# Sums of w_out in parts within block 0, and the copy of v with k^T v within the second product of block 1

## Chip, cores and metric

The kernel runs on one core of a Trainium2 chip. The metric is the device time of one execution in microseconds (us). A core has five engines with a queue of instructions each: TensorE (PE in the profile; its weight loads are PEld), VectorE (DVE), ScalarE (ACT), GpSimd (POOL) and SyncE (SP). Each works through its own queue in order and waits for the others by semaphores. Transfers are issued by SP and POOL here and run on 16 DMA engines.

## What is computed

A linear attention with cosine weights, whose result goes through a feed-forward layer with a quick gelu. Everything arrives and leaves as float32; the kernel computes the products in bf16.

```python
# q, k, v: 8 batches x 8 heads x 576 positions x 64
def phi(x, c, s):
    r = np.maximum(x, 0.0)
    return np.concatenate([r * c, r * s], axis=-1)
q_p = phi(q, cos_w, sin_w)
k_p = phi(k, cos_w, sin_w)
kv = np.einsum('bhsf,bhsd->bhfd', k_p, v)
z = np.sum(k_p, axis=2)
num = np.einsum('bhsf,bhfd->bhsd', q_p, kv)
den = np.einsum('bhsf,bhf->bhs', q_p, z)[..., None] + 1e-06
attn_out = num / den
# x: attn_out as 4608 tokens x 512; w_in 512 x 2048, w_out 2048 x 512
h = x @ w_in
g = h * (1.0 / (1.0 + np.exp(-1.702 * h)))
return g @ w_out
```

## The kernel before

A block is one batch: 576 positions, of which 512 are its main tokens and 64 its tail. The tails of all blocks are gathered and computed at the end. The scheduler is off: each engine runs its instructions in the order in which the program writes them, so a line's place in the source is its place in the queue of its engine.

For each block b there are these steps:

- `trig_q(c)` (L176) makes the q features of one of five chunks of positions, a cosine and a sine half each, on VectorE (or ScalarE with `act`), from the loaded `qf` into `qn`; `qturn_dma(c)` (L217) turns the chunk into `qT` by a DMA transpose that SP issues.
- `trig(kr, kf, j)` (L161) makes the k features of one of nine slices `j`, two halves each, from the loaded `kf` into `kr`: on VectorE, on ScalarE with `act=True`, and with `act="sin"` the sine half alone on ScalarE.
- `vcopy(i0, i1, act)` (L187) casts v from `vf` to bf16 in `vt`, for the pairs of heads i0 to i1, on VectorE or on ScalarE.
- `kv_next()` (L589) is k^T v: 72 matmuls on TensorE from `kr` and `vt` into a PSUM tile `at`, and its evacuation to `kvs` on VectorE (`kv_evac`, L243).
- `x_next(b, c)` (L759) makes x of one chunk: `num_mm` (8 matmuls from `qT` and `kvs`), `num_div` (three VectorE instructions ending in `xn`), and `xturn_dma`, a DMA transpose from SP into `xT` (chunks 0 to 3) or `xt` (the tail).
- `mm1(b, fc)` (L373) is the first product for 128 of the 2048 hidden columns: 4 matmuls of 128x512 on TensorE, then a gelu on ScalarE into `g`. Its PSUM tiles come from the pool `pmm` of four banks, so mm1 of column group n writes where column group n-4 was, and waits for that one's gelu.
- The second product of blocks 1 to 7 uses seven smaller products in place of eight (`PRODUCTS`, L473: p1, p2, p6, p5, p7, p3, p4, of 16 matmuls in each of two steps). It needs sums of parts of w_out (`wsum`: t1, t2, t3, nt4, made once in `w_sums`, L438) and sums of parts of g for each block (`sums`: s1 to s4, made in `g_sums`, L458, for half h = 0 or 1 of the column groups). s3 of half h reads the gelus 4h to 4h+3, the others those and 8+4h to 11+4h. `wino_after` (L549) keeps or joins results after each product and stores them.

Block 0 uses the plain second product (`mm2`, L414). While it runs, block 1's q, k and v are prepared (L716 to L728); then `start_block(1)` runs mm1 of the first five column groups of block 1, and `w_sums()` stands after it (L765). The loop over blocks 1 to 7 (L767) runs mm1 over the other column groups with the preparation of block b+1 written in between, and then the second product. Within that product, for b = 1, `vcopy()` is written after step 1, k^T v of the next block after step 3, and the five `x_next` after steps 4, 5, 6, 8 and 10. For b > 1 k^T v is written between mm1 of groups 13 and 14.

w_out is loaded in four groups of 4 of its 16 row blocks by POOL (`load_wout`, L150). k and v of a later block are loaded by SP (`load_kv`, L146), q by SP too (`load_q`, L133). Block 2's loads are issued at L727 and L728; block 3's q is issued in the loop of block 1, after block 2's qT transposes, and its k and v after the fourth `x_next`.

Of the kernel before, what the change touches and what calls it, by code (L numbers as in the profile page):

```python
# [15 lines left out]
SUB = mybir.AluOpType.subtract  # L16
# [4 lines left out]
def kernel(  # L21
# [9 lines left out]
    nc = tc.nc  # L31
# [29 lines left out]
    kf, vf = [one.tile([128, NI, S], F32, name=n) for n in ("kf", "vf")]  # L61
# [47 lines left out]
    kr = one.tile([128, NS, NI, 128], BF16, name="kr")  # L109
# [17 lines left out]
    def load_chunks(t, src, b, eng):  # L127
        eng.dma_start(out=t[:, 0:2048].rearrange("p (h e) -> p h e", h=H),
                      in_=src[b, :, 0:512, :].rearrange("h (p c) d -> p h (c d)", c=4))
        eng.dma_start(out=t[0:64, 2048:2560].rearrange("p (h e) -> p h e", h=H),  # L130
                      in_=src[b, :, 512:S, :].rearrange("h p d -> p h d"))

    def load_q(b, eng=nc.gpsimd):  # L133
        load_chunks(qf, q, b, eng)
# [11 lines left out]
    def load_kv(b):  # L146
        load(kf, k, b, nc.sync)
        load(vf, v, b, nc.sync)
# [12 lines left out]
    def trig(dst, src, j, act=False, eng=nc.vector):  # L161

        i = src[:, :, ts(j, 64)]
        for cs, w in enumerate((cosw, sinw)):
            o = dst[:, j, :, ts(cs, 64)]
            if act is True or (act == "sin" and cs == 1):
                nc.scalar.activation(o, i, AF.Relu, scale=w[:, j:j + 1])
            else:
                eng.tensor_scalar(o, i, 0.0, w[:, j:j + 1], op0=MAX, op1=MUL)  # L169
# [6 lines left out]
    def trig_q(c, act=False):  # L176
        n = 128 if c < 4 else 64
        i = chunk(qf, c)
        for cs, w in enumerate((cosw, sinw)):
            o = qn[0:n, c, :, ts(cs, 64)]  # L180
            sc = w[0:n, NS + c:NS + c + 1]
            if act:
                nc.scalar.activation(o, i, AF.Relu, scale=sc)
            else:
                nc.vector.tensor_scalar(o, i, 0.0, sc, op0=MAX, op1=MUL)  # L185

    def vcopy(i0=0, i1=NI, act=False):  # L187
        o = vt[:, :, i0:i1, 0:64].rearrange("p j i e -> p i j e")
        i = vf[:, i0:i1].rearrange("p i (j e) -> p i j e", e=64)
        if act:  # L190
            nc.scalar.activation(o, i, AF.Copy)
        else:
            nc.vector.tensor_copy(o, i)  # L193
# [23 lines left out]
    def qturn_dma(c):  # L217
        n = 128 if c < 4 else 64
        nc.sync.dma_start_transpose(out=qT[:, :, c * 128:c * 128 + n],
                                    in_=qn[0:n, c].rearrange("p h f -> p (h f)"))  # L220
# [3 lines left out]
    def kv_open(i0=0, i1=NI, n=65):  # L224
        t = pat.tile([128, 2, 512], F32, name="at")
        for i in range(i0, i1):
            st["kv", i] = t[:, :, ds((i - i0) * n, n)]
        st["ps", i0] = t[:, :, 0:(i1 - i0) * n]
        if i0 == 0:
            st["kvs"] = small.tile([128, 2, NI, VW], BF16, name="kvs", bufs=2)  # L230

    def kv_mm(i0, i1, rhs, col, n):
        for i in range(i0, i1):
            for j in range(NS):
                for hh in range(2):
                    r = slice(hh * 64, hh * 64 + 64)
                    nc.tensor.matmul(st["kv", i][:, hh, ds(col, n)], kr[r, j, i, :], rhs(r, i, j),  # L237
                                     start=(j == 0), stop=(j == NS - 1))
# [4 lines left out]
    def kv_evac(i0, i1, n=65):  # L243
        o = st["kvs"][:, :, i0:i1, 0:n]
        nc.vector.tensor_copy(o, st["ps", i0].rearrange("p hh (i e) -> p hh i e", e=n))  # L245
# [85 lines left out]
    def x_open(b):  # L331
        x[b] = xpool.tile([128, KC, MT], BF16, name="xT")
# [40 lines left out]
    def mm1(b, fc):  # L373
        mm1_part(b, fc, 0, MT)
        gelu(fc)
# [38 lines left out]
    def mm2(b, t, lo, hi, c0=0, c1=d_model, end=False):  # L414
# [6 lines left out]
        if hi == FC:  # L421
# [10 lines left out]
    wt = {n: wsum[:, i].rearrange("p (f d) -> p f d", f=HF)  # L432
          for i, n in enumerate(("t1", "t2", "t3", "nt4"))}
    wq = {(k, n): w_out_sb[:, ts(k, HF), ts(n, HD)] for k in range(2) for n in range(2)}
    sg = {n: sums[:, i].rearrange("p (f t) -> p f t", f=HF)
          for i, n in enumerate(("s1", "s2", "s3", "s4"))}

    def w_sums():  # L438
        tt = nc.vector.tensor_tensor
        tt(wt["t1"], wq[0, 1], wq[0, 0], op=SUB)  # L440
        tt(wt["t2"], wq[1, 1], wt["t1"], op=SUB)
        tt(wt["t3"], wq[1, 1], wq[0, 1], op=SUB)
        tt(wt["nt4"], wq[1, 0], wt["t2"], op=SUB)

    def main_blk(i, qd):

# [11 lines left out]
    def g_sums(names, h, of=MAIN):  # L458

        tt = nc.vector.tensor_tensor  # L460
        a_blk, to = of
        o = {n: to[n][:, ts(h, 4)] for n in to}
        for n in names:
            if n == "s1":
                tt(o[n], a_blk(1, h), a_blk(1, h + 2), op=ADD)
            elif n == "s2":
                tt(o[n], o["s1"], a_blk(0, h), op=SUB)  # L467
            elif n == "s3":
                tt(o[n], a_blk(0, h), a_blk(1, h), op=SUB)  # L469
            else:  # L470
                tt(o[n], a_blk(0, h + 2), o["s2"], op=SUB)
# [114 lines left out]
    def vt_rhs(r, i, j):  # L586
        return vt[r, j, i, 0:65]

    def kv_next():  # L589
        kv_open()  # L590
        kv_mm(0, 4, vt_rhs, 0, 65)
        kv_evac(0, 4)

    def start_block(b):
# [120 lines left out]
    load_wout(3)  # L715
    for j in range(NS):  # L716
        trig(kr, kf, j)
    for fc in range(8, FC):
        mm1(0, fc)
    mm1_tail_first(0)  # L720
    mm1_tail_first(1)
    for c in range(5):
        trig_q(c, act=(c > 2))
        qturn_dma(c)
    vcopy(0, 2)
    vcopy(2, 4, act=True)
    load_q(2, nc.sync)  # L727
    load_kv(2)  # L728
    for g in range(2):
# [2 lines left out]
    for t in range(4):  # L732
        mm2(0, t, 8, 12)
    kv_next()
    mm2(0, 0, 12, 16)
    x_open(1)
# [15 lines left out]

    def kv_operands(b):
        for j in range(NS):
            trig(kr, kf, j)
        if b > 2:
            vcopy()

    def x_next(b, c):  # L759
        num_mm(c)  # L760
        num_div(c)
        xturn_dma(b, c)


    w_sums()  # L765

    for b in range(1, B):  # L767
        nb = b + 1 if b + 1 < B else None
        f0 = 5 if b == 1 else 0
        for fc in range(f0, FC):  # L770
            if nb is not None and fc == f0:
                for c in range(5):
                    trig_q(c)
                    qturn_dma(c)
            if nb is not None and fc == f0 + 1:
                kv_operands(nb)

                if nb + 1 < B:
                    load_q(nb + 1, nc.sync)
            if fc == 12:  # L780
                g_sums(("s3",), 0)
                g_sums(("s3",), 1)
                g_sums(("s1", "s2", "s4"), 0)
            if fc == 14 and nb is not None and b > 1:
                kv_next()
            mm1(b, fc)
        if nb is not None:
            x_open(nb)
            if b > 1:
                x_next(nb, 0)  # L790
            g_sums(("s1", "s2"), 1)
            at = {2 * p + 1: [p + 1] for p in range(4)} if b > 1 else {4: [0], 5: [1], 6: [2], 8: [3], 10: [4]}
            wino_open()
            for p in range(7):
                for c in range(2):
                    wino_mm(p, c)
                    s = 2 * p + c
                    if c == 1:
                        wino_after(b, p)
                    if s == 3 and b == 1:  # L800
                        kv_next()
                    for c2 in at.get(s, ()):
                        x_next(nb, c2)
                        if c2 == 3 and nb + 1 < B:
                            load_kv(nb + 1)
                    if s == 1:
                        g_sums(("s4",), 1)
                        if b == 1:
                            vcopy()
            continue  # L810
        for fc in range(FC):
            mm1_tails(fc)
            if fc == 0:
                g_sums(("s1", "s2", "s4"), 1)
        for h in range(2):
            g_sums(("s1", "s2"), h, TAIL)
        g_sums(("s3",), 0, TAIL)
        g_sums(("s3",), 1, TAIL)
        wino_open()
        for p in range(7):  # L820
            for c in range(2):
                wino_mm(p, c, TAIL)
            wino_after(None, p, end=True)
            if p == 1:
                g_sums(("s4",), 0, TAIL)
                g_sums(("s4",), 1, TAIL)
        wino_open(last=True)
        for p in range(7):
            for c in range(2):
                wino_mm(p, c)  # L830
                if p == 6:
                    wino_last(b, c)
            wino_after(b, p, end=True)
# [30 lines left out]
```

## Time and profile before

| What | Value |
|---|---|
| median of 3 runs | 286.86 us (286.69 to 287.23) |
| time of the profiled execution | 288.89 us |
| span of the profiled execution | 287.2 us |
| mean granted TensorE clock | 0.987 |
| busy: PE, DVE, ACT, POOL | 273.7, 185.7, 128.3, 41.4 us |
| bytes read from and written to HBM | 36.70 MB, 9.44 MB |

The span runs from the first to the last instruction of the trace; all moments named below count from its start. Block 1's second product begins at 65.54 us, block 2's mm1 at 88.66 us.

How to read the lines. A timeline line gives start, duration, engine, source line, operation, the tiles written and read, their shapes, a count, and in brackets the idle time of the engine before it with what ended it. A line of waits gives who waited for whom, the sum in us, how often, and the longest. A line of windows gives the stretch, its length, busy time and count of PE, PEld, DVE, ACT and POOL, then the granted clock, the busy share of the DMA engines and GB/s. A line of DMA issues gives tiles, issuing queue, count, size and the time from issue to landing (a median where several are grouped). L numbers are lines of the kernel before.

### The profile page before, as it was taken

What the parts mean: (1) busy time and instruction counts of PE and PEld (TensorE: products, weight loads), DVE (VectorE), ACT (ScalarE), POOL (GpSimd) and SP (SyncE); (2) the same over time, 40 slices, a digit from 0 to 9 for tenths busy, and PEclk for the clock granted to TensorE, in tenths of its full rate; (3) what the DMA queues carried; (4) which work ended last, traced back from release to release, by engine and by line L of the source; (5) the groups of instructions that cost most, each with busy time, mean ns of one, the idle gap of its engine ahead of it and who ended that gap; (6) DMA issues with size and microseconds to landing.
All of it is one profiled execution on the core that took longest, in us unless ns stands there. A gap on an engine that the chain in (4) does not pass through costs nothing.

```text
span 287.2 us, 6573 instructions
## 1 busy us (share of the span) xinstructions
PE 273.7 (95%) x2700; PEld 191.5 (67%) x2700; DVE 185.7 (65%) x451; ACT 128.3 (45%) x225; POOL 41.4 (14%) x70
## 2 busy tenths in 40 slices
PE   8999999996698989999999999999999999999995
PEld 2675645854594559757975797579757975568884
DVE  4835434799585798796779678967897711516111
ACT  6967543672014722364236413641374137773221
POOL 5680003200112001300130013001300130000320
PEclk9999999999599999999999999999999999999999
DMA  7999999999349999999699979987994430000143
GB/s 238 245 212 295 270 257 204 350 296 202 103 64 251 290 183 168 292 264 236 112 305 221 217 148 314 256 212 107 290 279 54 109 119 2 0 0 2 47 138 110
DMA packets 73661, 53.57 MB, mean 187 GB/s; under 512 B 52736, under 2 KB 63488, under 8 KB 73632
## 3 DMA queue, kind: packets, MB, share of 16 engines
q1 hardware_dynamic: 67504, 36.97, 56.8%
q0 software_dynamic: 6128, 16.19, 20.2%
q8 instruction: 21, 0.34, 0.5%
q14 instruction: 8, 0.07, 0.1%
HBM read 36.70 MB, written 9.44 MB: 161 GB/s over the span
## 4 chain that ended last, share of the span: by engine, by line
PE 77%; DVE 10%; DMA 9%; issue 1%; ACT 1%; POOL 0%; DVEq 0%; SPq 0%
PE mm L502 32%; PE mm L365 29%; DMA kf<-in_k_dram 5%; PE mm L396 4%; PE mm L419 4%; PE at L237 3%; DVE kr L169 3%; PE at L310 3%; DMA sums<-in_v_dram 2%; DMA out_dram<-ysb 2%; DVE qn L185 1%; DVE vt L193 1%; DVE sums L469 1%; PE mm L388 1%; DVE sums L467 1%
## 5 line engine op out<-in xcount | busy, mean ns | idle before, releaser
L365 PE MATMUL mm<-xT,w_in 128*128 128x512 bf16 (+1 forms) x592 | 113.7, 349 | 1.5 <-DMA xT<-xn 1.4
L371 ACT ACTIVATE g<-mm 128x512 bf16<-128x512 f32 x128 | 75.6, 598 | 41.2 <-PE mm L365 41.2
L365 PEld LDWEIGHTS <-w_in 128*128 128x128 bf16 x592 | 60.1, 113 | 48.3 <-issue 1.7
L502 PEld LDWEIGHTS <-sums 128*128 128x128 bf16 x448 | 42.6, 98 | 5.0
L508 POOL DMA_DIRECT2D out_dram<-ysb x24 | 17.5, 729 | 165.2 <-DVE inv L323 96.8
L502 PE MATMUL mm<-wsum,sums 128*128 128x256 bf16 x336 | 40.9, 276 | 0.0
L502 PEld LDWEIGHTS <-g 128*128 128x128 bf16 x336 | 32.2, 98 | 3.8
L169 DVE TENSOR_SCALAR kr<-kf,cosw 128x256 bf16<-128x256 f32 x69 | 24.2, 350 | 10.0 <-DMA kf<-in_k_dram 10.0
L325 DVE TENSOR_TENSOR xn<-at,inv 128x512 bf16<-128x512 f32 x39 | 27.0, 691 | 1.3
L502 PE MATMUL mm<-w_out_sb,g 128*128 128x256 bf16 x224 | 26.4, 272 | 0.0
L169 DVE TENSOR_SCALAR kr<-kf,sinw 128x256 bf16<-128x256 f32 x68 | 23.1, 339 | 0.0
L517 ACT ACTIVATE kept_u<-mm 128x512 f32<-128x512 f32 (+1 forms) x9 | 4.9, 550 | 33.7 <-PE mm L502 16.9
L517 ACT ACTIVATE kept_p<-mm 128x512 f32<-128x512 f32 (+1 forms) x17 | 9.7, 572 | 22.6 <-PE mm L502 22.6
L185 DVE TENSOR_SCALAR qn<-qf,cosw 128x512 bf16<-128x512 f32 (+1 forms) x33 | 16.3, 494 | 4.0 <-DMA qf<-in_q_dram 4.0
L321 DVE TENSOR_SCALAR den<-at 128x8 f32<-128x8 f32 x36 | 5.9, 163 | 17.4 <-PE at L310 17.4
L310 PEld LDWEIGHTS <-qT 128*128 128x128 bf16 x312 | 14.6, 98 | 3.4 <-issue 1.0
L569 ACT ACTIVATE ysb<-mm 128x512 f32<-128x512 f32 x6 | 3.6, 597 | 29.3 <-PE mm L502 29.3
L310 PE MATMUL at<-kvs,qT 128*128 128x65 bf16 x312 | 15.9, 194 | 0.8 <-DVE kvs L245 0.8
L237 PEld LDWEIGHTS <-kr 64*128 64x128 bf16 x576 | 10.3, 98 | 8.2 <-issue 6.5
L185 DVE TENSOR_SCALAR qn<-qf,sinw 128x512 bf16<-128x512 f32 (+1 forms) x33 | 15.6, 473 | 0.0
L237 PE MATMUL at<-vt,kr 64*128 64x65 bf16 x504 | 9.7, 197 | 5.5 <-DVE vt L193 5.5
L419 PE MATMUL mm<-w_out_sb,g 128*128 128x512 bf16 x64 | 14.8, 379 | 0.0
(120 smaller groups left out, 264.7 us busy)
## 6 DMA issues: line engine op xcount, KB each, us to landing
kf<-in_k_dram SPq DMA_DIRECT2D x6, 1152.0 KB, 6.5
vf<-in_v_dram SPq DMA_DIRECT2D x6, 1152.0 KB, 11.8
qf<-in_q_dram SPq DMA_DIRECT2D x6, 1024.0 KB, 6.5
out_dram<-ysb POOLq DMA_DIRECT2D x24, 256.0 KB, 6.5
w_out_sb<-in_moe_w_out_dram POOLq DMA_DIRECT2D x4, 512.0 KB, 17.6
kf<-in_k_dram POOLq DMA_DIRECT2D x1, 1152.0 KB, 13.2
vf<-in_v_dram POOLq DMA_DIRECT2D x1, 1152.0 KB, 20.7
w_in<-in_moe_w_in_dram POOLq DMA_DIRECT2D x2, 512.0 KB, 10.2
```

The source lines that it names most:

```text
L169: eng.tensor_scalar(o, i, 0.0, w[:, j:j + 1], op0=MAX, op1=MUL)
L185: nc.vector.tensor_scalar(o, i, 0.0, sc, op0=MAX, op1=MUL)
L237: nc.tensor.matmul(st["kv", i][:, hh, ds(col, n)], kr[r, j, i, :], rhs(r, i, j), start=(j == 0), stop=(j == NS - 1))
L310: nc.tensor.matmul(ps[:, h // 4, ds((h % 4) * 65, 65)], qT[:, h, ts(c, 128)], kvs_of(h), start=not eps_too, stop=(not eps_too or h % 4 == ...
L325: nc.vector.tensor_tensor(xn, pv[:, :, :, 0:64], inv.unsqueeze(3).to_broadcast([128, 2, 4, 64]), op=MUL)
L365: nc.tensor.matmul(hp[fc][:, t0:t1], wcol(kc, fc), x[b][:, kc, t0:t1], start=(kc == 0), stop=(kc == KC - 1))
L371: nc.scalar.activation(gT[fc // 4][:, fc % 4], hp.pop(fc), AF.Gelu_apprx_sigmoid)
L396: nc.tensor.matmul(hps[:, 64:B * 64], wcol(kc, fc), xt[:, kc, 64:B * 64], start=(kc == 0), stop=(kc == KC - 1))
L419: nc.tensor.matmul(yp[b, t, c0][:, c0:c1], w, w_out_sb[:, fc, c0:c1], start=(fc == 0), stop=(fc == FC - 1))
L502: nc.tensor.matmul(bank[to][c], lhs, rhs, start=opens, stop=(fc == HF - 1), skip_group_check=True)
L508: eng.dma_start(out=dst[:, 2 * i + c0:2 * i + c1, ts(n, HD)], in_=t[:, c0:c1])
L517: nc.scalar.activation(o, i, AF.Identity)
```

## The change

The four sums of w_out are no longer made in one go after `start_block(1)`. t1 is made behind block 0's k features; t2, t3 and nt4 are made in two halves, the first behind block 1's q features, the second behind VectorE's half of the copy of v. In block 1 (b == 1) the two s3 sums and the k features of block 2 move behind mm1 of group 7, with the sine half of every second slice on ScalarE; s4 of half 0 leaves the place at group 12. The copy of v is written ahead of the second product, half on ScalarE and half on VectorE. k^T v stays behind step 3, with the two s4 sums around its evacuation. The `x_next` stand behind steps 5, 6, 7, 8 and 10. Blocks 2 to 7 keep their order.

```diff
-    def w_sums():
+    def w_sum_1():
+        nc.vector.tensor_tensor(wt["t1"], wq[0, 1], wq[0, 0], op=SUB)
+
+    def w_sums(h):
+
         tt = nc.vector.tensor_tensor
-        tt(wt["t1"], wq[0, 1], wq[0, 0], op=SUB)
-        tt(wt["t2"], wq[1, 1], wt["t1"], op=SUB)
-        tt(wt["t3"], wq[1, 1], wq[0, 1], op=SUB)
-        tt(wt["nt4"], wq[1, 0], wt["t2"], op=SUB)
+        o = {n: wt[n][:, ts(h, 4)] for n in wt}
+        w = {n: wq[n][:, ts(h, 4)] for n in wq}
+        tt(o["t2"], w[1, 1], o["t1"], op=SUB)
+        tt(o["t3"], w[1, 1], w[0, 1], op=SUB)
+        tt(o["nt4"], w[1, 0], o["t2"], op=SUB)
...
-    def kv_next():
+    def kv_mm_next():
         kv_open()
         kv_mm(0, 4, vt_rhs, 0, 65)
+
+    def kv_next():
+        kv_mm_next()
         kv_evac(0, 4)
...
     for j in range(NS):
         trig(kr, kf, j)
+    w_sum_1()
     for fc in range(8, FC):
         mm1(0, fc)
...
     for c in range(5):
         trig_q(c, act=(c > 2))
         qturn_dma(c)
+    w_sums(0)
     vcopy(0, 2)
     vcopy(2, 4, act=True)
+    w_sums(1)
     load_q(2, nc.sync)
     load_kv(2)
...
     def kv_operands(b):
         for j in range(NS):
-            trig(kr, kf, j)
+            trig(kr, kf, j, act="sin" if b == 2 and j % 2 else False)
         if b > 2:
             vcopy()
...
-    w_sums()
 
     for b in range(1, B):
...
-            if nb is not None and fc == f0 + 1:
+            if nb is not None and fc == f0 + 1 and b > 1:
                 kv_operands(nb)
 
                 if nb + 1 < B:
                     load_q(nb + 1, nc.sync)
-            if fc == 12:
+            if fc == 8 and b == 1:
+                load_q(nb + 1, nc.sync)
                 g_sums(("s3",), 0)
                 g_sums(("s3",), 1)
-                g_sums(("s1", "s2", "s4"), 0)
+                kv_operands(nb)
+            if fc == 12:
+                if b > 1:
+                    g_sums(("s3",), 0)
+                    g_sums(("s3",), 1)
+                g_sums(("s1", "s2", "s4") if b > 1 else ("s1", "s2"), 0)
...
             g_sums(("s1", "s2"), 1)
-            at = {2 * p + 1: [p + 1] for p in range(4)} if b > 1 else {4: [0], 5: [1], 6: [2], 8: [3], 10: [4]}
+            if b == 1:
+                vcopy(2, 4, act=True)
+                vcopy(0, 2)
+            at = ({2 * p + 1: [p + 1] for p in range(4)} if b > 1 else
+                  {5: [0], 6: [1], 7: [2], 8: [3], 10: [4]})
...
-                    if s == 3 and b == 1:
-                        kv_next()
                     for c2 in at.get(s, ()):
                         x_next(nb, c2)
                         if c2 == 3 and nb + 1 < B:
                             load_kv(nb + 1)
-                    if s == 1:
+                    if s == 1 and b > 1:
                         g_sums(("s4",), 1)
-                        if b == 1:
-                            vcopy()
+                    if s == 3 and b == 1:
+                        kv_mm_next()
+                        g_sums(("s4",), 0)
+                        kv_evac(0, 4)
+                        g_sums(("s4",), 1)
```

## The prediction

> **What bounds the kernel now.** I read the page first, then the list of waits and the timeline of PE between 40 and 122 us, then windows by stage for the clock, and last VectorE, SP and the DMA landings of that stretch. The page gives the frame: PE works almost throughout.
>
> ```profile
> PE 273.7 (95%) x2700; PEld 191.5 (67%) x2700; DVE 185.7 (65%) x451; ACT 128.3 (45%) x225; POOL 41.4 (14%) x70
> PE   8999999996698989999999999999999999999995
> PEclk9999999999599999999999999999999999999999
> ```
>
> PE is full from the third slice on, except slices 10 and 11 (each slice is 7.18 us, so 65 to 79 us), and slice 11 is the only one with a low granted clock. From 118 us on the chain of waits is PE alone and each block takes 28.57 us (one block's p1 to the next). So a change to blocks 0 and 1 can only act on what stands before 118 us. The waits of PE between 24 and 125 us, and PE's timeline around them:
>
> ```profile
> PE at L237 <- DVE vt L193: 5.5, 2, 4.8
> PE mm L365 <- DMA xT<-xn: 1.4, 1, 1.4
> PE at L310 <- DVE kvs L245: 0.8, 1, 0.8
> ```
> ```profile
> 65.54 3.66 PE L502 MATMUL mm<-w_out_sb,g 128*128 128x256 bf16 x32
> 74.05 2.16 PE L237 MATMUL at<-vt,kr 64*128 64x65 bf16 x72 [4.85 <-DVE vt L193]
> 76.14 1.89 PE L502 MATMUL mm<-wsum,sums 128*128 128x256 bf16 x8
> ...
> 88.66 12.25 PE L365 MATMUL mm<-xT,w_in 128*128 128x512 bf16 x56 [1.41 <-DMA xT<-xn]
> ```
> ```profile
> 66.00:74.00 8.00, 3.20 (x30) 2.72 (x28) 7.86 (x16) 0.94 (x2) 0.00 (x0) 0.84 0.84 201
> 74.00:90.00 16.00, 14.54 (x199) 12.26 (x199) 11.37 (x29) 2.06 (x4) 3.00 (x4) 0.87 0.47 91
> 106.00:119.00 13.00, 13.00 (x144) 11.72 (x142) 9.86 (x23) 1.79 (x3) 2.18 (x3) 1.00 0.97 212
> ```
>
> After four steps of the second product (p1, p2) PE stands for 4.85 us until VectorE has copied v. Then it runs slowly: the 72 k^T v matmuls take 2.16 us (1.19 between the same marks of the chain in later blocks), the first step behind them 1.82 (0.87 elsewhere). The granted clock, the column before the last two, is 0.84 and 0.87 there and 1.00 later. VectorE is why:
>
> ```profile
> 53.98 1.22 DVE L440 TENSOR_TENSOR wsum<-w_out_sb 128x2048 bf16<-128x2048 bf16 x1
> ...
> 58.65 0.48 DVE L185 TENSOR_SCALAR qn<-qf,cosw 128x512 bf16<-128x512 f32 x1
> ...
> 72.64 1.35 DVE L193 CAST vt<-vf 128x2304 bf16<-128x2304 f32 x1
> ```
>
> From 53.98 to 73.99 it never idles: w_sums 4.67 us, trig_q 3.96, the 18 kr instructions 4.7, the sums of g 5.3, the copy 1.35. What the stall costs: the second product of block 1 is 14 steps of 0.873, k^T v 1.19 and five num_mm of 0.24, together 14.6 us; begun at 65.54 it would end at 80.2. The trace ends it at 87.25 (88.66 less 1.41). So 7.05 us are at stake: 5.0 of standing (from the end of step four at 69.03) and 2.05 of low clock.
>
> **The change, part by part.** *w_sums out of block 1 (VectorE).* The four sums leave the 4.67 us before trig_q. t1 goes behind block 0's kr work, which ends at 31.3; it needs groups 0 and 1 of w_out, landed at 14.14 + 14.8 = 28.9 and 14.69 + 16.6 = 31.3. It takes 1.22 us, to 32.6; VectorE idles until q lands at 35.38, so it costs nothing (2.8 us of cover). The first half of t2, t3, nt4 stands behind trig_q, which ends at 37.8; group 2 lands at 19.52 + 18.4 = 37.9; three instructions of 128x1024 at 0.61 (the row of L465) end at 39.8, before v lands at 40.84: nothing. The second half needs group 3, the last of the four loads:
>
> ```profile
> w_out_sb<-in_moe_w_out_dram POOLq DMA_DIRECT2D x1, 512.0 KB, 19.6
> ```
>
> Issued at 23.73, it lands at 43.33; 1.9 us of sums end at 45.25, and the evacuation of kvs behind them, for which num_mm waits, began at 45.24 before. Cost 0 to 0.1 here, and if group 3 came 1 us later, 1 us at that place; I take 0 because, as follows, block 1 waits for a landing anyway.
>
> *trig_q, then s3, then kr.* trig_q can start at 54.07 (q landed at 46.84 + 7.2 = 54.04) and ends at 58.0. The first s3 sum runs to 58.6; the second waits for gelu 7, which ends at 59.44, and is done at 60.1. kr needs the k of block 2, whose issue on SP and time to landing are:
>
> ```profile
> 48.57 0.64 SPq L125 DMA_DIRECT2D kf<-in_k_dram  x1
> ```
> ```profile
> kf<-in_k_dram SPq DMA_DIRECT2D x1, 1152.0 KB, 12.1
> ```
>
> It lands at 48.57 + 12.1 = 60.67, which w_sums hid before (first kr at 62.61). Now two engines wait for it: VectorE 0.6 us (hidden), and ScalarE, where four sine halves stand between gelu 7 and gelu 8. ScalarE's Relu instructions of this shape followed each other at 0.40 us (L167, 6.88 to 12.46), so they run 60.71 to 62.31, and gelu 8, which started at 59.76, ends at 62.9. Behind it queue all later gelus, and mm1 has four banks: mm1(12), due at 62.27, needs gelu 8's. PE stands some 0.65 us and mm1 ends at 66.2 instead of 65.54. Were k there at 59.4, this would be nothing; each further microsecond of k is a microsecond.
>
> [...]
>
> *kr, sums, copy.* VectorE's 14 kr instructions (0.263 apart) end at 64.4. s1, s2 of half 0 need gelu 11 (ScalarE catches up at 0.5 per gelu: 64.4) and end at 65.8; s1, s2 of half 1 need gelu 15 (67.05) and end at 68.5. The copy is split: ScalarE's half 1.17 us from 66.95 to 68.1 (v lands at 49.38 + 14.4 = 63.8), VectorE's 0.76 from 68.4 to 69.15. PE finishes p2 at 66.2 + 3.5 = 69.7: 0.55 us of cover, so the 4.85 us and the low clock go. keep("p1") is pushed to 68.1 behind ScalarE's copy, and its bank is wanted at 70.9. The two s4 sums now stand around the kvs evacuation: join to 70.4, s4 to 71.0, kvs to 71.7, s4 to 72.3; kvs is wanted at 72.64, s4 at p3 (77.1). No stall.
>
> *num_mm one step later.* PE: k^T v to 70.9, p6 to 72.64, then num_mm 0 to 3 one step (1.11 us) apart, the fourth ending at 76.2, the product at 80.85. xn of the fourth ends 1.33 later (82.48 to 83.81 before): 77.55. SP's transposes take 1.2 to 1.3 us each from 74.25, so the fourth is issued at 78.15, or at 79.2 if the third takes 2.28 again. Landing 3.9 later (84.6 to 88.5 before): 82.05 to 83.1. I take 82.5 for mm1 of block 2, against 88.66.
>
> *SP.* block 2's five qT transposes are issued from 55.0 instead of 59.6, behind k and v in the same queue; load_q(3) follows, wanted at 79. The loads of block 3 follow the fourth xT transpose as before, so block 2 keeps its own two waits (0.6 and 0.8 us).
>
> **Sum.** 7.05 recovered, less 0.65 (gelu 8) and 0.25 more of waiting for xT: 6.15, that is 88.66 - 82.5. The profiled execution took 288.89 us with a span of 287.2; the median of the runs is 286.86, 0.3 below the span. I subtract from the median: 280.7 us.
>
> **Rivals.** *The transposes slow k (slower).* If the DMA engines shared their time between the early qT transposes and k and v, k's remaining 5.7 us at 55.0 would double (five transposes are 6.5 us of work at 1.3 each): k at 66.4. ScalarE's queue would then hold gelu 8 until 68.6, PE would stand 6.4 us at mm1(12), longer than the 4.85 that brought the low clock (another 2.05): 8.45 lost against 7.05 won, and with 0.25 for xT 288.5 us. It decides from a k some 4 us late. Against it: block 2's xt transpose, issued at 87.38 behind v (86.72), landed 11.8 later at 99.2, and v at 98.9; the quickest took 2.3. The queue kept its order. [...] *xT comes late.* With four transposes one step apart, the longest landing in the xT rows (6.2) would give 78.15 + 6.2 + 0.15 = 84.5 and 282.7 us. *More is won.* If k of block 3 lands after 6.0 as in the next block instead of 9.5, block 2's waits of 0.6 and 0.8 go too: 279.3. Against it, the same three stores run beside it. *It doesn't do what it says.* If VectorE's half of the copy were still last, by more than the 0.55, PE would stand for the rest; for no gain at all it would have to be 6 us late, and no row on its way is so uncertain, except k.
>
> **Chances.** Forecast (280.0 to 281.8) 0.65; xT late or a similar wait of 1 to 2 us 0.14; more won 0.12; slower by the transposes 0.06; no gain 0.03. The range takes the first three but for their edges: 279.1 to 283.0. A measurement of this kernel tells 0.2% (0.6 us) from no change: faster 0.91, same 0.02, slower 0.07.
>
> **What would show it.** PE's timeline: no wait before the k^T v of block 1, and 72 matmuls in 1.2 us; a short wait at L365 inside block 1's mm1; clock 1.00 in the slice at 74 us; mm1 of block 2 near 82.5 with a wait for xT of 1 to 2 us. ScalarE: four L167 rows that start at 60.7 behind a wait for kf. VectorE: wsum between 31 and 46 us. Wrong would be kf landing past 62, a long wait at L365, or vt still as PE's releaser.

## The result and the profile after

The changed kernel takes 282.69 us in the median of four runs (282.08 to 283.27), the kernel before 287.05 beside it (286.69 to 287.61): a ratio of 0.9846 with a 95% interval of 0.9818 to 0.9875, that is 4.4 us less (3.6 to 5.2). The profiled execution has a span of 280.3 us. Two repeats of the same kernel gave ratios of 0.9823 (0.9770 to 0.9877) and 0.9827 (0.9775 to 0.9880). Disturbed runs are left out of all comparisons; the profiled execution of both these repeats was one, so they give times and no trace.

The page of the changed kernel, TensorE's share and the granted clock by slice:

```profile
PE 271.2 (97%) x2700; PEld 190.0 (68%) x2700; DVE 184.5 (66%) x450; ACT 130.6 (47%) x230; POOL 41.4 (15%) x70
...
PE   7899999999989999999999999999999999999994
...
PEclk9999999999999999999999999999999999999999
```

The hole in slices 10 and 11 is gone and the clock with it; what is left is an 8 in the twelfth, at 77 to 84 us (each slice is 7.0 us). PE's waits between 24 and 125 us, then its timeline:

```profile
PE mm L365 <- DMA xT<-xn: 1.2, 1, 1.2
PE at L310 <- DVE kvs L245: 0.8, 1, 0.8
PE mm L365 <- ACT g L371: 0.4, 1, 0.4
PE at L237 <- DVE vt L193: 0.2, 1, 0.2
```
```profile
62.67 3.61 PE L365 MATMUL mm<-xT,w_in 128*128 128x512 bf16 x16 [0.37 <-ACT g L371]
66.12 3.66 PE L507 MATMUL mm<-w_out_sb,g 128*128 128x256 bf16 x32
69.71 1.26 PE L237 MATMUL at<-vt,kr 64*128 64x65 bf16 x72
...
82.20 12.25 PE L365 MATMUL mm<-xT,w_in 128*128 128x512 bf16 x56 [1.18 <-DMA xT<-xn]
94.63 1.26 PE L237 MATMUL at<-vt,kr 64*128 64x65 bf16 x72 [0.18 <-DVE vt L193]
...
98.50 0.40 PE L310 MATMUL at<-kvs,qT 128*128 128x65 bf16 x8 [0.75 <-DVE kvs L245]
```

k^T v now follows the fourth step with no wait. The row of 72 k^T v matmuls lasts 1.26 us where it lasted 2.16, and block 1's second product takes 14.9 us (66.12 to 81.02, which is 82.20 less 1.18) in place of 21.7. (A step of it is 8 matmuls, as the row of 32 for four steps shows, and a product 16.) In its stead stand small waits: 0.37 in mm1, for a gelu, and in block 2 0.18 and 0.75 (0.61 and 0.76 before). The clock by windows:

```profile
66.00:74.00 8.00, 8.00 (x146) 7.01 (x145) 5.38 (x10) 2.90 (x5) 0.74 (x1) 1.00 0.88 229
74.00:82.00 8.00, 7.02 (x86) 6.12 (x82) 7.46 (x20) 1.20 (x2) 1.51 (x3) 1.00 0.71 108
```

VectorE's rows that carry the moved work, and below them ScalarE's and SP's:

```profile
31.68 1.23 DVE L439 TENSOR_TENSOR wsum<-w_out_sb 128x2048 bf16<-128x2048 bf16 x1
...
43.20 0.69 DVE L446 TENSOR_TENSOR wsum<-w_out_sb,wsum 128x1024 bf16<-128x1024 bf16 x1 [1.76 <-DMA w_out_sb<-in_moe_w_out_dram]
...
45.29 0.70 DVE L245 CAST kvs<-at 128x520 bf16<-128x520 f32 x1 [0.20 <-PE at L237]
...
60.43 0.35 DVE L169 TENSOR_SCALAR kr<-kf,cosw 128x256 bf16<-128x256 f32 x1 [0.22 <-DMA kf<-in_k_dram]
...
68.29 0.75 DVE L193 CAST vt<-vf 128x1152 bf16<-128x1152 f32 x1
```
```profile
60.43 1.71 ACT L167 ACTIVATE kr<-kf,sinw 128x256 bf16<-128x256 f32 x4 [0.95 <-DMA kf<-in_k_dram]
```
```profile
54.98 12.36 SPq L219 DMA_TRANSPOSE qT<-qn  x5
```

The second half of the sums does wait for the last load of w_out (1.76 us), and is still done 0.2 before the evacuation of kvs, which waits for PE. ScalarE stands 0.95 us for k with gelu 8 behind it. The copy ends at 69.04, 0.67 ahead of its use.

### The profile page after: what moved, and what is told of

It reads as the page before. It is cut to its first block, busy times and chain, and to the rows that moved or that the text cites. A ratio compares the mean times of both kernels' runs of the same rounds, so it can differ in the third digit from the quotient of the medians.

```text
span 280.3 us, 6580 instructions
## 1 busy us (share of the span) xinstructions
PE 271.2 (97%) x2700; PEld 190.0 (68%) x2700; DVE 184.5 (66%) x450; ACT 130.6 (47%) x230; POOL 41.4 (15%) x70
## 4 chain that ended last, share of the span: by engine, by line
PE 81%; DMA 11%; DVE 4%; SPq 1%; ACT 1%; issue 1%; POOL 0%; DVEq 0%
PE mm L507 34%; PE mm L365 31%; DMA kf<-in_k_dram 8%; PE mm L396 4%; PE mm L419 4%; PE at L237 3%; PE at L310 3%; DMA sums<-in_v_dram 2%; DVE kr L169 2%; PE mm L388 1%; PE mm L205 0%; ACT kr L167 0%; DVE vt L193 0%; SPq L219 0%; DVE sums L474 0%
## 5 line engine op out<-in xcount | busy, mean ns | idle before, releaser
L507 PE MATMUL mm<-wsum,sums 128*128 128x256 bf16 x336 | 40.1, 272 | 0.0
L169 DVE TENSOR_SCALAR kr<-kf,sinw 128x256 bf16<-128x256 f32 x64 | 21.7, 339 | 0.0
L474 DVE TENSOR_TENSOR sums<-g 128x1024 bf16<-128x1024 bf16 x14 | 9.2, 681 | 8.8 <-ACT g L371 8.8
L470 DVE TENSOR_TENSOR sums<-g 128x1024 bf16<-128x1024 bf16 x14 | 9.6, 687 | 7.9 <-ACT g L371 7.8
```

The source lines that it names most:

```text
L507: nc.tensor.matmul(bank[to][c], lhs, rhs, start=opens, stop=(fc == HF - 1), skip_group_check=True)
```

## The experiments

The first three are made from the kernel before, the others from the changed one. Times are medians; ratios are to the kernel before, run beside them, with their 95% intervals.

**The kernel before, again** (no edit).

> The kernel before, unchanged, to see its spread. Theory A: the low TensorE clock behind the 4.85 us stall is granted only in some executions; then most executions have a mean clock of 1.00 and a span about 2 us below 287.2 (near 285.1, time near 286.9), and a few have 0.987 and near 288.9. Rival B: the low clock belongs to every execution, the profiled one of 288.89 us was slower for another reason; then all show a clock near 0.987, and those of 286.9 too.

Measured: 287.11 us, span of the profiled execution 286.3. Theory A fell: in all 12 executions, and in 21 of the kernel before run beside them, the mean clock was 0.985 to 0.994, never 1.00. So the low clock belongs to the kernel before. It comes in two sizes: with the 28 executions run beside the later experiments there are 61, of which 38 had a mean clock of 0.985 to 0.988 and 23 one of 0.991 to 0.994, with medians of 287.48 and 286.70 us. Both traces are of the first kind. But its size and what follows differ from one execution to the next. PE's waits of this second trace:

```profile
PE at L237 <- DVE vt L193: 4.8, 1, 4.8
PE mm L365 <- DMA xT<-xn: 0.4, 1, 0.4
PE at L310 <- DVE kvs L245: 0.3, 1, 0.3
```

The stall is the same, the waits behind it are 0.76 us together, where the first trace had 1.41 + 0.61 + 0.76 = 2.78. That first profiled execution (288.89 us) was not a typical one: it stood 1.8 above the median. This second one (288.04) stood 0.9 above it.

**Idle matmuls in the stall.** `idle(20)` runs 20 matmuls of 512 columns on a tile `warm`; nothing reads their result.

```diff
                     if s == 3 and b == 1:
+                        idle(20)
                         kv_next()
```

> The kernel before with 20 idle matmuls of 512 columns (4.3 us) on TensorE in the stall ahead of k^T v: the stall stays, the low clock should go. It prices the low clock by itself. If all of its 2.05 to 2.7 us counts: 287.1 - 2.3 = 284.8 us, clock 1.00. If a faster product is partly given back as waits for xT and for k of block 3 (0.44 and 0.32 us in the repeated trace of the kernel before, 1.18 and 0.93 in the changed one): some 1.0 us less than 287.1, 286.1 us, with those waits grown to 1.2 and 0.9. If the clock isn't lowered by the stall: no change and a clock of 0.99.

Measured: 285.40 us beside 287.40, ratio 0.9934 (0.9903 to 0.9965), clock 0.998 to 1.000 in all 12 executions.

```profile
69.08 4.48 PE L581 MATMUL mm<-warm 128*128 128x512 bf16 x20
74.08 1.26 PE L237 MATMUL at<-vt,kr 64*128 64x65 bf16 x72 [0.53 <-DVE vt L193]
```

v comes as late as before (74.08), but PE has not been idle, and k^T v takes 1.26. So the low clock by itself costs 2.0 us of the median, with an interval of 1.0 to 2.8. The 2.05 of the prediction lies in it, and so, at its edge, does the 1.0 of a cost that is half given back as waits. This trace doesn't decide between them: its wait for xT is 1.22 us, between the 1.41 and 0.44 of the two traces before. Three of the twelve executions took 287.2 to 287.4 us at a full clock, and no trace shows why.

**Only the sums moved** (`w_sum_1()`, `w_sums(0)` and `w_sums(1)` defined and placed as in the change, nothing else).

> The kernel before with only the sums of w_out moved into block 0. VectorE: q features to 58.0, k features wait for k (60.4) and end at 65.2, the eight sums at 70.4, the copy at 71.7; PE stands from 69.0 to 71.7, 2.7 us instead of 5.0. Theory A (low clock only in some executions, none typical): 286.9 - 2.3 = 284.6 us. Rival B (low clock in every execution of the kernel before, and gone with a stall of 2.7): 282.5 us. Rival C (the moved sums are hidden by the wait for k): no gain, 286.9.

Measured: 285.18 us, ratio 0.9911 (0.9877 to 0.9944), between A and no gain, with A's 284.6 inside the interval. In its trace k landed at 61.6 instead of 60.7, so the stall was longer than forecast:

```profile
73.10 1.36 PE L237 MATMUL at<-vt,kr 64*128 64x65 bf16 x72 [3.90 <-DVE vt L193]
```

The rest goes with the clock. Nine of the eleven executions had a mean clock of 0.986 to 0.994 and took 284.33 to 286.67 us; two had 1.00 and took 282.75 and 283.69, near the 282.5 that B said. What set those two apart, no trace shows.

**The sums put back** (the change without that part).

```diff
...
-    w_sum_1()
...
-    w_sums(0)
...
-    w_sums(1)
...
+    w_sums()
+
     for b in range(1, B):
```

> The changed kernel with the sums of w_out back in block 1 behind start_block(1), all else as changed. VectorE: q features to 62.6, s3 63.8, 14 k features 67.5, s1 and s2 70.3, its half of the copy 71.05; p2 ends at 69.7, so PE stands 1.35 us at k^T v and the time is 282.7 + 1.35 = 284.0 us. Rival: moving the sums is where the gain is; then PE stands some 4 us again, 286.5 or more.

Measured: 283.46 us, ratio 0.9868 (0.9820 to 0.9915), clock 0.999 to 1.000 in five of six. The rival fell: without the moved sums the rest of the change still takes off 4.0 us of 287.46. PE's waits in this trace:

```profile
PE mm L365 <- ACT g L371: 1.1, 1, 1.1
PE mm L365 <- DMA xT<-xn: 1.0, 1, 1.0
PE at L237 <- DVE vt L193: 0.9, 2, 0.5
```

The stall at k^T v of block 1 is 0.53 us; k came later here than in the first trace (the wait for gelu 8 is 1.1, not 0.4), which covers part of what the sums cost. By themselves the sums are worth 2.3 us, on top of the rest about 1, which the intervals of this kernel and the changed one don't tell from nothing: both fill the same hole.

**No sine half on ScalarE.**

```diff
-            trig(kr, kf, j, act="sin" if b == 2 and j % 2 else False)
+            trig(kr, kf, j)
```

> The changed kernel with all k features of block 2 on VectorE, none on ScalarE. The wait of 0.4 us at mm1 of group 12 goes; VectorE's k features end 1.05 us later (65.2), s2 at 67.9, its half of the copy at 68.65, and p2 ends at 69.07: no stall at k^T v, mm1 of block 2 at 81.65 instead of 82.20, 282.1 us. Rival: the sine halves are needed; the copy comes late by up to 1 us, PE waits for it at k^T v, 283.2 us.

Measured: 282.29 us, ratio 0.9811 (0.9776 to 0.9845); the changed kernel's own 282.69 and 282.43 cannot be told from it. In its profiled execution q of block 2 was issued at 48.3 and k features began at 62.79. The wait at mm1 is gone, and its place is the other end of the same chain:

```profile
PE mm L365 <- DMA xT<-xn: 1.8, 1, 1.8
PE at L237 <- DVE vt L193: 1.7, 1, 1.7
```

Whichever engine makes the k features, a late k reaches PE in this execution. The median is the one of the theory; the wait at k^T v is the one of the rival.

**x one step earlier.**

```diff
-                  {5: [0], 6: [1], 7: [2], 8: [3], 10: [4]})
+                  {4: [0], 5: [1], 6: [2], 7: [3], 10: [4]})
```

> The changed kernel with the five x_next one step earlier again (behind steps 4, 5, 6, 7 and 10), the fourth included. kvs is ready at 71.8, when step 4 ends, so no new wait; the fourth xn is ready 0.87 us earlier and the wait of 1.18 for xT falls to 0.3: 282.7 - 0.9 = 281.8 us. Rival: SP's transposes, not xn, set the pace (1.3 us each, one of them 2.2); then the wait shrinks by less than 0.4 and the time is 282.4 us.

Measured: 281.49 us, ratio 0.9804 (0.9762 to 0.9846). The interval overlaps that of the changed kernel, and the wait for xT did not shrink (1.3), so the mechanism I expected isn't shown. The fourth transpose was issued 0.8 us earlier after the product's start than in the changed kernel (11.3 us after it instead of 12.1), but the longest landing was 4.9 us instead of 3.9. Up to step 4 of block 1's product this kernel is the changed one, and its trace shows there what a later landing of k does. ScalarE's row, then PE's waits:

```profile
61.65 1.70 ACT L167 ACTIVATE kr<-kf,sinw 128x256 bf16<-128x256 f32 x4 [2.29 <-DMA kf<-in_k_dram]
```
```profile
PE mm L365 <- ACT g L371: 1.7, 1, 1.7
PE mm L365 <- DMA xT<-xn: 1.3, 1, 1.3
```

k was issued at 48.97 and landed 12.7 later, and PE stood 1.71 us for gelu 8, not 0.37. Block 2's mm1 then starts 1.36 us later than in the changed kernel (83.56 and 82.20), but block 3's only 0.20 later (112.13 and 111.93): the waits of 0.18 and 0.75 in block 2 are not there.

**The changed kernel again**, twice.

> The changed kernel, unchanged, for its spread and a second trace. Theory: k of block 2 lands between 60.4 and 62.8 us from one execution to another, which the kernel before hid (first k feature at 62.6) and this one doesn't; so its spans spread over some 2 us, the median is near 281.0 (time 282.7), and the wait at mm1 of group 12 is longer than 0.37 us where k lands later than 60.4. Rival: the spread comes from elsewhere; the second trace has k at 60.4 and a span over 281 all the same.

> The changed kernel, unchanged, once more for a second readable trace and its median. Theory: in most executions q and k of block 2 are issued near 47.7 us on SP (so in five of eight traces so far) and not at 46.7; k then lands near 61.6, ScalarE's sine halves and gelu 8 come 1.2 us later than in the first trace, and the wait at mm1 of group 12 is near 1.6 us. Median 282.6 us. Rival: that wait is 0.4 us whenever it is looked at, and the gain against 7.05 was lost elsewhere.

Measured: 282.43 us (ratio 0.9823) and 281.96 (0.9827). With the first four that makes 14 executions, from 280.85 to 285.52, half of them between 281.9 and 283.0; 13 had a clock of 0.998 to 1.000. The slowest had 0.993; one execution with the sums put back (0.994, 286.31 us) and one with k loaded by POOL (0.994, 285.68) are like it, and whether PE stood in them no trace shows. The medians are those of the two theories, but their mechanism is not shown: a late k is seen in x one step earlier (a wait of 1.71) and in the kernel with the sums put back (1.05), and not in the one trace of the changed kernel.

**k of block 2 loaded early by POOL.**

```diff
     w_sum_1()
+    load(kf, k, 2)
...
     load_q(2, nc.sync)
-    load_kv(2)
+    load(vf, v, 2, nc.sync)
```

> The changed kernel with k of block 2 loaded by POOL behind the last group of w_out, as soon as block 1's k features are made, instead of by SP behind q. k then lands before 50 us. Theory (the late k costs the changed kernel 0.4 us in its profiled execution and about 1 us in the median one): no wait for kf on ScalarE or VectorE in block 1, no wait at mm1 of group 12, 281.7 us and a narrower spread. Rival: the wait moves to another landing (q of block 2, or block 1's qT transposes, which now share the engines with this load); 282.7 us or more.

Measured: 282.94 us, ratio 0.9854 (0.9808 to 0.9899): the rival. The wait at gelu 8 is gone, but block 1's qT transposes, beside which this load now runs, took SP 13.88 us (10.46 in the changed kernel), and PE waited for them ahead of block 1:

```profile
PE at L310 <- DMA qT<-qn: 0.8, 1, 0.8
```

**k first on SP.** The loads go k, q, v instead of q, k, v, and VectorE makes k's features, then s3, then q's.

```diff
-    load_q(2, nc.sync)
-    load_kv(2)
+    load(kf, k, 2, nc.sync)
+    load_q(2, nc.sync)
+    load(vf, v, 2, nc.sync)
...
-            trig(kr, kf, j, act="sin" if b == 2 and j % 2 else False)
+            trig(kr, kf, j)
...
+            if fc == f0 and b == 1:
+                kv_operands(nb)
-            if nb is not None and fc == f0:
+            if nb is not None and fc == f0 and b > 1:
...
-                load_q(nb + 1, nc.sync)
                 g_sums(("s3",), 0)
                 g_sums(("s3",), 1)
-                kv_operands(nb)
+                for c in range(5):
+                    trig_q(c)
+                    qturn_dma(c)
+                load_q(nb + 1, nc.sync)
```

> The changed kernel with SP's loads for block 2 in the order k, q, v in place of q, k, v, the k features first on VectorE (all of them, none on ScalarE), then s3, then the q features. The same bytes in the same queue behind the same transposes, so block 1's qT isn't touched. Theory (the late k costs the median 1.2 to 1.7 us): k lands near 55, VectorE's half of the copy ends at 68.6 to 69.1 and p2 at 69.07, no wait at mm1 of group 12 and at most 0.2 at k^T v: 282.6 - 1.3 = 281.3 us. Rival: q, now second, comes as late as k did and holds s1, s2 and the copy by more than 1 us: 282.6 us or more, with the wait at k^T v.

Measured: 281.19 us, ratio 0.9772 (0.9730 to 0.9814), five executions within 280.56 to 281.38. PE in its trace:

```profile
65.60 3.66 PE L507 MATMUL mm<-w_out_sb,g 128*128 128x256 bf16 x32
...
81.46 12.25 PE L365 MATMUL mm<-xT,w_in 128*128 128x512 bf16 x54 [0.96 <-DMA xT<-xn]
```

The product begins at 65.60, where it began before the change (65.54), and there is no wait at gelu 8 or at k^T v.

**Both, k first and x earlier** (the two diffs together).

> k_first with the five x_next behind steps 4, 5, 6, 7 and 10 as in x_earlier. If the two add up: 281.3 - 1.0 = 280.3 us, and it is the fastest of all. If SP's transposes set the pace of xT, no more than k_first: 281.3 us.

Measured: 280.83 us, ratio 0.9765 (0.9720 to 0.9810): the lowest median, not to be told from k first alone, and between the two numbers expected. In its profiled execution, the fastest of them (279.44 us, span 277.7), all that PE waited for between 24 and 125 us was this:

```profile
PE at L310 <- DVE kvs L245: 0.3, 1, 0.3
```

## Why the prediction was right, and where it was off

**The way and the place were right.** The forecast was 280.7 us in a range of 279.1 to 283.0; measured were 282.69, and in the repeats 282.43 and 281.96. All three lie in the range, but above the 280.0 to 281.8 that had most of the chance. Against the profiled execution its moments hold to 0.4 us: second half of the sums done before kvs is wanted, q features from 54.03 (54.07), k features from 60.43 (60.71), mm1's end and the product's start at 66.12 (66.2), VectorE's half of the copy done at 69.04 (69.15), no wait at k^T v, mm1 of block 2 at 82.20 (82.5).

**The low clock: right in kind.** 2.05 us from rows of one execution; 2.0 by the idle matmuls (1.0 to 2.8), and present in every execution of the kernel before, though not in one size: PE worked 4.2 us at a clock of 0.50 behind the stall in the first trace (74.05 to 78.2) and 5.4 us in the second (from 74.67; an estimate from its mean of 0.62 in 74 to 82 us), which by itself would cost 2.1 and 2.7.

**The transposes that might slow k: didn't.** Issued 4.6 us earlier, at 54.98, the five kept SP busy for 12.36 us instead of 8.01, but k took 12.0 us to land, as before (12.1). That is what two traces show.

**ScalarE's sines: right in kind.** Four rows 0.40 apart, as the rows had it, and the gelus behind them go on at 62.05 without a table load: both this trace and the one before have two of them, of 1.28 us each, at 0.8 and 2.5 us, and none later.

**The size was off by 1.8 us**, 6.15 forecast and 4.4 measured (5.1 and 5.0 by the ratios of the repeats). The part inside the trace held: from the profiled execution before to the one after, 288.89 to 282.08, 6.8 us went, more than the 6.15, and PE's wait at mm1(12) was 0.37 where 0.65 was put down. The step that failed is the sum's base, "I subtract from the median". The 6.15 is the difference of two starts of block 2's mm1, the first of them read from an execution that took 288.89 us, and it was subtracted from a median of 286.86. The median beside the changed kernel was 287.05, 1.84 below that execution, and the profiled execution of the changed kernel lies 0.6 below its own median: 6.8 less 1.84 and 0.6 is the 4.4. Subtracted from its own execution the sum would have given 282.7, and that it meets the measured 282.69 is partly luck: a sum that was 0.7 too small met an execution 0.6 below the median.

What the first execution had that a typical one has not is shown in part. It had 2.78 us of waits behind the stall, the second trace 0.76; the changed kernel has 2.11. I kept block 2's own waits "as before". Against the second trace the account closes: the product 22.3 to 14.9, 7.4 won, 1.35 more waits behind it, 6.05, and the spans are 286.3 and 280.3. But that execution, too, stood 0.9 above its median, and both traces have the larger of the two sizes of the low clock.

**A late k.** The prediction took k at 60.67 from one execution and put no spread on it. q of block 2 leaves SP when block 1's five transposes are through, at 46.7 to 47.0 in the two traces of the kernel before and the first of the changed one, but at 47.7 to 48.3 in five other traces of kernels that keep this order (only the sums moved, idle matmuls, sums put back, no sine half, x earlier); k then lands from 61.2 on. The kernel before hid that up to 62.6, the first k feature, so its median doesn't feel it. The changed kernel doesn't hide it: PE's wait for gelu 8 was 0.37 in its profiled execution, 1.05 and 1.71 in two variants. Whether each further microsecond of k is a microsecond, as the prediction has it, is not shown: in x one step earlier 1.36 us at block 2's mm1 had become 0.20 at block 3's, though x was moved there as well. Taking the wait away (k first) brought 0.8 us against the changed kernel beside it (281.96 to 281.19) and a spread of 0.8 us; the intervals of the two ratios overlap, and the two profiled executions, of which the changed kernel's had k at 60.4, already differ by 0.7 (spans of 280.3 and 279.6). A later k can explain no more than what the changed kernel's median lies above its profiled execution, unless that execution had other waits that a typical one has not: 0.6 us in the first four executions, 0.2 over all 14. How much of it is k stays open, as there is no second trace of the changed kernel.

**The rivals.** In the profiled execution, more won (block 2's waits gone) and xT late didn't come. A wait of 1 to 2 us like the one that the chances name came at gelu 8 in two variants; in the changed kernel itself it was 0.37.

## What to carry to other kernels

When a change takes away the work that an engine did while a transfer was under way, the transfer's landing becomes a term of the sum: look in more than one execution for how far it moves, since the cover may have hidden its spread. A difference read from one profiled execution is to be subtracted from that execution, and from the median only after asking which of its waits a typical one has. And two ways to an earlier landing can differ: here the other order of loads within one queue gave 0.8 us by the medians, while the load moved to another queue gave nothing: block 1's transposes, which were wanted sooner, took 13.9 us of SP beside it, against 10.3 to 11.9 in the other traces.

## What the runs showed of the hardware

In these runs a long wait of PE cost more than its length. With the stall of 4.8 us of both its traces, the clock was lowered in all 61 executions of the kernel before (means of 0.985 to 0.994), at a price of 2.0 us (1.0 to 2.8); with only the sums moved, where the trace has a stall of 3.9 us, in nine of eleven (0.986 to 0.994); in x one step earlier, where the trace has a wait of 1.7 us, in none of six (0.998 to 1.000). No run here tries how short a wait is enough.

In the first trace of the kernel before, the lowered clock is 0.50, from 71.4 to 78.2 us. These 6.8 us begin 2.2 after PE stopped (69.20) and end 4.2 after it was at work again (74.05). The second trace has a mean of 0.95 in 66 to 74 us and 0.62 in 74 to 82; the trace with only the sums moved has 1.00 and 0.79, though PE was at work again from 73.10. If the lowered clock is 0.50 there too, these means stand for 6.9 and 3.4 us of it. An estimate from these lengths: 3.4 us at half clock take 0.006 off the mean of a span of 286 us, and 6.8 take 0.012, which fits the two sizes of the mean clock, near 0.994 and 0.988. Not all of it lies behind the stall: in the first trace the clock falls once more at 286.4 us, 2.8 after PE's last matmul (283.6), and the trace with only the sums moved has a mean of 0.991, 0.003 below what its 3.4 us take off.

SP's queue was held by its own transposes. Block 2's five qT transposes took 6.7 us of SP when issued from 61.2 us on (k first), 8.0 from 59.6 (the kernel before) and 12.4 from 55.0 (the changed kernel), with v, ahead of them in the queue, landing at 64.0, 63.8 and 63.4. The q load written behind them left at 67.98, 67.65 and 67.39, moments that no line of the program shows.
